# Agent attention with a maxout network: the first product over two PSUM tiles, w_out behind group 0's loads, and own orders for the last four groups

## The chip, the cores and the metric

The kernel runs on one core of a Trainium2 chip. The metric is device time in microseconds (us), the median of repeated executions. Engines are named as in the profile: PE is TensorE (PEld its weight loads), DVE is VectorE, ACT is ScalarE, POOL is GpSimd, SP is SyncE, which here only issues DMAs.

## The reference

Two stages. Attention goes through 49 agents for each of 4 batches of 12544 rows of 128 numbers; its result feeds a maxout network with 768 hidden units.

```python
def sm(a, b):
    s = scale * (a @ b.transpose(0, 2, 1))
    s = s - s.max(-1, keepdims=True)
    e = np.exp(s)
    return e / (e.sum(-1, keepdims=True) + 1e-09)
agent_v = sm(agents, k) @ v          # 49 x 128 for each batch
x = sm(q, agents) @ agent_v          # 50176 x 128 in all
h = np.maximum(np.maximum(x @ w1, x @ w2), x @ w3)
out = h @ w_out
```

## The kernel before

**What is multiplied.** The kernel never forms x. Because x is the agents' weights times agent_v, it multiplies agent_v (held turned, as avT) once for each batch with a wide matrix `wall`. That matrix has columns C21 to Dff for w2 - w1, C31 to C1O for w3 - w1 (but w3 - w2 for hidden block FI = 3), and from C1O for w1 times w_out, the linear part. The result of a batch is the tile G[b]. In `product` (lines 408 to 429) each product is a pair of matmuls, one for each half of the partitions, followed by a copy out of PSUM into G. A maximum of three is then rebuilt as a linear part plus sums of maxima: for each of the six hidden blocks f, `first(f)` (u) and `second(f)` (v) are matmuls of G with the exponentials of the scores (line 533). `relu_first` (a, line 548) runs on ACT and `max_second` (x, line 558) on DVE. For f = FI both steps are on ACT (lines 545 and 556), in the same PSUM tile. `out_linear` (line 563) and `out_hidden` (oc0f and oc1f for the two halves of a group, line 572) sum into an output tile, and `out_scale` (sc0, sc1, line 579) multiplies by the reciprocal row sums on its way to SBUF. `store` (line 586) writes a whole group once both scales are done.

**Stages.** The 392 row tiles are handled in 49 groups of eight. Batch 0's keys and values come first, alone, in twelve "early" groups (9 tiles each, the last two 4 each). Their last sums give avT for batch 0 (`normalise`, lines 402 and 403), and product 0 follows. Keys and values of batches 1 to 3 are worked on beside the query groups 0 to 35. Groups 36 to 48 have query work alone and use DMA transposes.

**Order.** Every step is put on one list with a key, by `at(key, fn, name, needs, ring, frees)`. `emit` sorts by key. A step whose needs are not yet done, or whose ring of PSUM buffers has none free, waits on a second list and is taken as soon as it can. What comes out is the program order of each engine's instructions, and each engine keeps to that order. The rings are "uv" (three tiles of two banks), "om" (two tiles of one bank) and "a" (three SBUF tiles). For a query group the keys are 6.0 times the group's number plus an entry of a table: KEY, BEGIN and BORDER for the groups with keys beside them, LATE for the rest (`table`).

**What the change touches.** `load_w_out` (line 193) is put at last_key - 29.85, right behind the load of query group 0 (last_key - 29.9) and ahead of the loads of key group 0 (at -24.6). w_out isn't in the ring of load tiles. `prep_w_out` (line 222) casts it on POOL at last_key - 3.24, behind the cast of query group 1 (last_key - 3.25). `linear_out` (line 240) and `linear_product_out` (line 249) copy the linear part out of PSUM on ACT. In `k_tail` batch 0's product has two pieces, (C31, C31 + 256, C1O) and (C21, C31). The first piece is one tile with two copies between its matmuls, and its key of last_key + 0.95 comes after the scores of group 0 at last_key + 0.94. The transposes of key group 0 (line 294) have last_key + 1.05, and the first u follows at last_key + 2.

Of the kernel before, what the change touches and what calls it, by code (L numbers as in the profile page):

```python
# [11 lines left out]
AF = mybir.ActivationFunctionType  # L12
# [4 lines left out]
def kernel(  # L17
# [18 lines left out]
    nc = tc.nc  # L36
    B, N, C = q.shape
    A = agents.shape[1]
    Dff = moe_w1.shape[1]
    scale = 1.0 / math.sqrt(C)  # L40
    P = 128
    NF = Dff // P
    H = 64
# [5 lines left out]
    NQ = B * NT // GT  # L49
# [46 lines left out]
        "oc11": 11.381, "oc13": 11.497,  # L96
    }
    PRODUCT_KEYS = (-8.717, -1.818)
    BEHIND = 2.6

    def table(s):
        if s + 1 in tails:
            return BORDER
        return BEGIN if s in tails and s < SB else KEY if s < SB else LATE
# [6 lines left out]
    def uv_tile(dtype=FP32):  # L111
        return psum.tile([P, 2, 512 if dtype == FP32 else 1024], dtype, tag="uv", bufs=3, name="uv_ps")
# [6 lines left out]
    def at(key, fn, name=None, needs=(), ring=None, frees=()):  # L119

        ops.append((key, len(ops), fn, name, needs, ring, frees))
# [46 lines left out]
    avT = const.tile([P, B, H], BF16, name="avT")  # L170
# [3 lines left out]
    r_ag = const.tile([P, B], FP32, name="r_ag")  # L174
# [25 lines left out]
    C21, C31, C1O = 0, Dff, 2 * Dff  # L200
    wall = const.tile([P, 2 * Dff + 3 * C], BF16, name="wall")
    nc.vector.memset(wall[:, C1O:], 0.0)
    WC = 2 * Dff + 2 * C
# [26 lines left out]
    linear = {}  # L230
# [4 lines left out]
    def prep_linear1(f):  # L235
        nc.tensor.matmul(linear["t"][:, :C], w1T[:, f, :], wo_bf[:, f, :], start=(f == 0),
                         stop=(f == NF - 1))

    def linear_out():
        nc.scalar.activation(wall[:, C1O + C:C1O + 2 * C], linear["t"][:, :C], AF.Copy)  # L240

    def linear_product():
        for h in range(2):
# [2 lines left out]
                             start=False, stop=True, skip_group_check=True)  # L246

    def linear_product_out():
        nc.scalar.activation(G[0][:, C1O:WC], linear["t"][:, C:3 * C], AF.Copy)

    def keep_busy(times):
        t = small_tile("m_ps")
# [4 lines left out]
    G = {}  # L257
# [6 lines left out]
    def k_group(b, t0, n, key, s):  # L264

        d = {}
        early = s is None
        K = None if early else table(s)
        if s == 0:
            key += BEHIND  # L270

# [110 lines left out]
    def k_tail(b, sum_key, keys, s):  # L382
        d = {}

        def reduce():
            w = KT // 2 * A
            t = Eacc[b]
            while w >= A:
                nc.gpsimd.tensor_tensor(out=t[:, :w], in0=t[:, :w], in1=t[:, w:2 * w], op=ALU.add)
                w = w // A // 2 * A  # L390
            nc.gpsimd.tensor_tensor(out=e_sum[:, :A], in0=t[:, :A], in1=t[:, KT * A - A:], op=ALU.add)

        def total():
            for h in range(2):
                nc.tensor.matmul(host[s][h * H:(h + 1) * H, :1], e_sum, ones[:, :1], start=True,
                                 stop=True, skip_group_check=True)

        def normalise():
            if s is None:

                r = last_tile["t"][:, :A]
                nc.vector.reciprocal(r, Vacc[b][:, A:])
                nc.vector.tensor_tensor(out=avT[:, b, :A], in0=Vacc[b][:, :A], in1=r, op=ALU.mult)
            else:
                nc.vector.reciprocal(r_ag[:, b:b + 1], host[s][:, :1])
            G[b] = work.tile([P, WC], BF16, tag="G", name="G")

        def product(c0, *ends):

            t = uv_tile().rearrange("p i c -> p (i c)")  # L410

            at0 = c0 if len(ends) == 1 else ends[0] - 512
            a = c0
            for z in ends:
                cuts = sorted({a, z} | {c for c in (at0 + 512, C1O) if a < c < z})
                for lo, hi in zip(cuts, cuts[1:]):
                    for h in range(2):


                        c = lo + (C if lo >= C1O and h == 0 else 0)  # L420
                        nc.tensor.matmul(t[h * H:(h + 1) * H, lo - at0:hi - at0], avT[:, b, :],
                                         wall[:, c:c + hi - lo], start=True, stop=True,
                                         skip_group_check=True)
                src = t[:, a - at0:z - at0]
                if s is None:
                    nc.vector.tensor_copy(out=G[b][:, a:z], in_=src)  # L426
                else:
                    nc.scalar.activation(G[b][:, a:z], src, AF.Copy, scale=r_ag[:, b:b + 1])
                a = z

        if s is not None:
            at(6.0 * (s - 1) + table(s - 1)["ke"] + 1.51, reduce, ("sum_e", b), [("kx", s - 1)])
            at(sum_key + 0.8, total, ("total", s), [("sum_e", b), ("ho", s)])
        at(sum_key + 0.81, normalise, ("normalise", b),
           [("ka", ("early", NT - last_size))] if s is None else [("total", s), ("ka", s - 1)])

        pieces = ((C31, C31 + 2 * P, C1O) if s is None else (C31, WC), (C21, C31))
        for i, piece in enumerate(pieces):
            at(keys[i], lambda piece=piece: product(*piece),
               ("product", b, i), [("normalise", b)], "uv", [("product", b, i)])  # L440


    def split(t0, t1, step):
# [10 lines left out]
    def q_group(s):  # L454
# [4 lines left out]
        d = {}  # L459
# [28 lines left out]
        def evacuate():  # L488
# [4 lines left out]
            else:  # L493
                nc.scalar.activation(qT, d["qT_ps"], AF.Copy)  # L494

        K = table(s)
        q_dma = s >= SB or s + 1 in tails

# [76 lines left out]
        def out_scale(o):  # L575
            if "out" not in d:
                d["out"] = work.tile([P, GT, C], FP32, tag="o_sb", bufs=3, name="o_sb")
            j, m = 2 * pairs[o][0], 2 * len(pairs[o])
            nc.vector.tensor_tensor(  # L579
                out=d["out"][:, j:j + m, :],  # L580
                in0=d["o", o].rearrange("p (j c) -> p j c", c=C),
                in1=d["r"][:, j:j + m].unsqueeze(2).to_broadcast([P, m, C]), op=ALU.mult)
# [8 lines left out]
        def put(name, fn, *needs, ring=None, frees=()):  # L591
            at(key + K[name] + (BEHIND if s == 0 and name in ("sum", "rec") else 0), fn, (name, s), needs,
               ring, frees)
# [30 lines left out]
        for f in range(NF):  # L624
            def each(fn, f=f):
                return lambda: fn(f)
            u, a, v, x = (n + str(f) for n in "uavx")
# [8 lines left out]
        for o in range(2):  # L636
            put(f"lin{o}", lambda o=o: out_linear(o), ("ex", s), *new_linear, ring="om",
                frees=[(f"sc{o}", s)])
            for f in range(NF):
                put(f"oc{o}{f}", lambda o=o, f=f: out_hidden(o, f), (f"lin{o}", s), (f"x{f}", s))  # L640
            put(f"sc{o}", lambda o=o: out_scale(o), ("rec", s),
                *[(f"oc{o}{f}", s) for f in range(NF)], *([("store", s - 3)] if s >= 3 else []))
        at(key + 12.2, store, ("store", s), [("sc0", s), ("sc1", s)])

    def ramp():

        at(KEY["lin1"] - 6, linear_tile, "linear", ["lin_a"], "om", ["lin_c"])
        keys = sorted(KEY[f"oc1{f}"] for f in range(NF))
        for f, key in enumerate(keys):
            at(key - 6, lambda f=f: prep_linear1(f), ("linear", f), ["linear"])  # L650
        key = 6 + KEY["a0"] + 0.01
        at(key, linear_out, "linear_out", [("linear", f) for f in range(NF)])
        at(key + 0.4, linear_product, "lin_b", ["linear_out"])
        at(6 + KEY["a1"] + 0.01, linear_product_out, "lin_c", ["lin_b", ("normalise", 0)])

# [1 line left out]
    last_key = KEY["u0"] - 2  # L659
# [3 lines left out]
    at(first_key - 6.5, load_weights)  # L663
    at(first_key + 30.2, prep_weights)
    at(first_key + 37.1, prep_linear0, "lin_a", (), "om", ["lin_a"])
    at(last_key - 29.85, load_w_out)
    at(last_key - 3.24, prep_w_out)
    fillers = []
    for g, n in enumerate(first_sizes):
        k_group(0, sum(first_sizes[:g]), n, first_key + 6.0 * g, None)  # L670

        if 4 <= g < len(first_sizes) - 3:
            fillers += [(first_key + 6.0 * g + 0.55, 3), (first_key + 6.0 * g + 1.3, 3)]
    k_tail(0, last_key, (last_key + 0.95, last_key + 1.02), None)
    for key, n in fillers + [(last_key + 0.9, 2), (KEY["u1"] + 0.01, 2),
                             (KEY["u3"] + 0.05, 2)]:
        at(key, lambda n=n: keep_busy(n), ("busy", key), (), "om", [("busy", key)])
    hosting = set()
    for b in range(1, B):
        for g in range(NK):  # L680
            s = (b - 1) * NT // GT + g
            hosting.add(s)
            k_group(b, g * KT, min(KT, NT - g * KT), 6.0 * s, s)
    for s, b in tails.items():
        assert s - 1 not in hosting
        k_tail(b, 6.0 * (s - 1) + table(s - 1)["ho"] + 0.001, [6.0 * s + PRODUCT_KEYS[i] for i in range(2)], s - 1)
    for s in range(NQ):
        q_group(s)
    ramp()

    with tc.manual_schedule():
# [31 lines left out]
```

## Time and profile before

| | |
|---|---|
| median of 8 executions | 463.36 us (463.18 to 463.49) |
| the profiled execution | 463.31 us |
| its span, first to last instruction | 461.5 us |
| granted TensorE clock | 0.999 of full |
| one group with keys beside it (68.72 to 77.08) | 8.36 us |
| one group without (424.88 to 432.74) | 7.86 us |
| last scale ends, end of the span | 457.92, 461.5 us |

The profile gives busy time for each engine. A busy PE is not a PE at its peak, since matmuls overlap and their ends are modelled. So the table gives starts: a step's cost in the stream is the distance from its start to that of the next one. Three stretches matter: up to about 41 us the loads of batch 0's keys and values set the pace; from 41 to about 62 us the query groups start up; then comes a regular run of groups to about 440 us, and the last groups drain.

### The profile page before, as it was taken

What the parts mean: (1) busy time and instruction counts of PE and PEld (TensorE: products, weight loads), DVE (VectorE), ACT (ScalarE), POOL (GpSimd) and SP (SyncE); (2) the same over time, 40 slices, a digit from 0 to 9 for tenths busy, and PEclk for the clock granted to TensorE, in tenths of its full rate; (3) what the DMA queues carried; (4) which work ended last, traced back from release to release, by engine and by line L of the source; (5) the groups of instructions that cost most, each with busy time, mean ns of one, the idle gap of its engine ahead of it and who ended that gap; (6) DMA issues with size and microseconds to landing.
All of it is one profiled execution on the core that took longest, in us unless ns stands there. A gap on an engine that the chain in (4) does not pass through costs nothing.

```text
span 461.5 us, 13320 instructions
## 1 busy us (share of the span) xinstructions
PE 437.4 (95%) x5457; PEld 274.4 (59%) x5462; DVE 402.2 (87%) x510; ACT 396.6 (86%) x460; POOL 171.8 (37%) x179
## 2 busy tenths in 40 slices
PE   2598899999999999999999999999999999999996
PEld 2476466666656666666656666666656555555554
DVE  3255899999989999999989999999988999999995
ACT  3365989999899899898998998999999999999982
POOL 2244964644462535445273355363240101100000
PEclk9999999999999999999999999999999999999999
DMA  8999999999999999998987999996776485644122
GB/s 314 408 410 391 349 343 355 334 343 253 311 318 289 289 291 311 293 260 254 319 304 265 274 302 323 300 249 191 159 148 184 126 196 150 182 116 125 60 94 91
DMA packets 82632, 118.53 MB, mean 257 GB/s; under 512 B 56391, under 2 KB 57867, under 8 KB 82571
## 3 DMA queue, kind: packets, MB, share of 16 engines
q1 hardware_dynamic: 82368, 117.59, 83.8%
q8 instruction: 42, 0.69, 0.6%
q14 instruction: 19, 0.16, 0.1%
q10 hardware_dynamic: 203, 0.10, 0.1%
HBM read 78.74 MB, written 25.69 MB: 226 GB/s over the span
## 4 chain that ended last, share of the span: by engine, by line
PE 80%; DMA 8%; DVE 5%; ACT 4%; issue 1%; SPq 0%; POOL 0%; DVEq 0%; ACTq 0%
PE uv_ps L533 34%; PE o_ps L572 29%; PE o_ps L563 6%; DMA st<-in_k_dram 5%; PE m_ps L486 4%; DVE r L558 4%; PE m_ps L507 3%; ACT a_sb L548 2%; DMA st<-in_q_dram 2%; DMA st<-in_v_dram 2%; PE m_ps L323 2%; PE m_ps L312 1%; PE m_ps L521 1%; DVE o_sb L579 0%; DVE G L426 0%
## 5 line engine op out<-in xcount | busy, mean ns | idle before, releaser
L558 DVE TENSOR_TENSOR r<-uv_ps,a_sb 128x1024 bf16<-128x1024 f32 x245 | 297.6, 1221 | 16.3 <-PE uv_ps L533 7.6
L548 ACT ACTIVATE a_sb<-uv_ps 128x1024 bf16<-128x1024 f32 x245 | 241.0, 1028 | 15.4 <-PE uv_ps L533 13.9
L533 PE MATMUL uv_ps<-e_q,G 49*128 49x512 bf16 (+3 forms) x1248 | 186.8, 368 | 2.5 <-ACT a_sb L548 0.3
L572 PE MATMUL o_ps<-wo_bf,r 128*128 128x128 bf16 x2352 | 175.2, 220 | 0.2 <-DVE r L558 0.2
L572 PEld LDWEIGHTS <-r 128*128 128x128 bf16 x2352 | 137.7, 98 | 40.1 <-issue 38.1
L533 PEld LDWEIGHTS <-G 49*128 49x128 bf16 x1248 | 57.7, 93 | 64.7 <-issue 32.7
L342 POOL TENSOR_TENSOR Eacc<-Eacc,e_k 128x441 f32<-128x441 f32 (+1 forms) x30 | 30.5, 1017 | 124.8 <-ACT e_k L317 124.8
L579 DVE TENSOR_TENSOR o_sb<-o_ps,recips 128x512 f32<-128x512 f32 x98 | 67.5, 689 | 9.1 <-PE o_ps L572 6.3
L481 POOL CAST q_bf<-st 128x1024 bf16<-128x1024 f32 x49 | 50.9, 1042 | 61.7 <-DMA qT<-q_bf 59.1
L556 ACT ACTIVATE r<-uv_ps 128x1024 bf16<-128x1024 f32 x49 | 50.2, 1025 | 17.9 <-PE uv_ps L533 17.7
L280 POOL CAST k_bf<-st 128x1152 bf16<-128x1152 f32 (+2 forms) x45 | 50.4, 1121 | 29.3 <-DMA st<-in_k_dram 23.2
L545 ACT ACTIVATE uv_ps<-uv_ps 128x1024 f32<-128x1024 f32 x49 | 49.6, 1013 | 0.2
L563 PE MATMUL o_ps<-G,e_q 128*128 128x256 bf16 x196 | 38.0, 276 | 0.0
L287 POOL CAST v_bf<-st 128x1152 bf16<-128x1152 f32 (+1 forms) x33 | 37.5, 1136 | 0.6 <-DMA st<-in_v_dram 0.6
L513 ACT ACTIVATE e_q<-m_ps 128x512 bf16<-128x512 f32 x49 | 29.9, 610 | 0.5 <-PE m_ps L507 0.5
L285 ACT ACTIVATE v_bf<-st 128x1152 bf16<-128x1152 f32 (+1 forms) x12 | 12.9, 1073 | 13.2 <-DMA st<-in_v_dram 13.1
L563 PEld LDWEIGHTS <-e_q 128*128 128x128 bf16 x196 | 12.5, 97 | 18.7 <-issue 18.0
L300 DVE COPY kT<-uv_ps 128x1152 bf16<-128x1152 bf16 (+1 forms) x14 | 9.9, 709 | 14.6 <-PE uv_ps L294 14.6
L486 PEld LDWEIGHTS <-q_bf 128*128 128x128 bf16 x264 | 14.9, 98 | 13.0 <-issue 11.1
L492 DVE COPY qT<-m_ps 128x1024 bf16<-128x1024 bf16 x32 | 21.8, 682 | 0.0
L486 PE MATMUL m_ps<-ident,q_bf 128*128 128x128 bf16 x264 | 20.4, 220 | 0.3 <-POOL q_bf L481 0.3
L507 PE MATMUL m_ps<-qT,agT 128*64 128x512 bf16 (+3 forms) x104 | 19.9, 388 | 0.7 <-ACT qT L494 0.7
(71 smaller groups left out, 227.4 us busy)
## 6 DMA issues: line engine op xcount, KB each, us to landing
st<-in_q_dram SPq DMA_DIRECT2D x46, 512.0 KB, 4.7
out_dram<-o_sb SPq DMA_DIRECT2D x46, 512.0 KB, 3.7
st<-in_k_dram SPq DMA_DIRECT2D x40, 576.0 KB, 6.7
st<-in_v_dram SPq DMA_DIRECT2D x40, 576.0 KB, 7.4
st<-in_k_dram SPq DMA_DIRECT2D x3, 512.0 KB, 6.2
st<-in_v_dram SPq DMA_DIRECT2D x3, 512.0 KB, 7.2
wst<-in_moe_w_dram SPq DMA_DIRECT2D x3, 384.0 KB, 10.5
st<-in_q_dram SPq DMA_DIRECT2D x2, 384.0 KB, 4.6
```

The lines of the kernel that those rows point to most:

```text
L280: nc.gpsimd.tensor_copy(out=d["kb"][:, :n, :], in_=d["k"][:, :n, :])
L287: nc.gpsimd.tensor_copy(out=d["vb"][:, :n, :], in_=d["v"][:, :n, :])
L481: nc.gpsimd.tensor_copy(out=d["qb"], in_=d["q"])
L486: nc.tensor.transpose(t[:, j * P:(j + 1) * P], d["qb"][:, j, :], ident)
L533: nc.tensor.matmul(t[:, h, j0 * P:j1 * P], G[b][h * H:h * H + A, col + f * P:col + (f + 1) * P], d["e"][h * H:h * H + A, j0 * P:j1 * P], s ...
L545: nc.scalar.activation(u, u, AF.Relu)
L548: nc.scalar.activation(a_sb[f], u, AF.Relu)
L556: nc.scalar.activation(r, v_ps[f], AF.Relu)
L558: nc.vector.tensor_tensor(out=r, in0=v_ps[f], in1=a_sb[f], op=ALU.max)
L563: nc.tensor.matmul(t[:, i * 2 * C:(i + 1) * 2 * C], d["e"][:, jj * P:(jj + 1) * P], G[batch[jj]][:, C1O:C1O + 2 * C], start=(i == 0), stop ...
L572: nc.tensor.matmul(t[:, c:c + C], r_sb[f][:, h, jj * P:(jj + 1) * P], wo_bf[:, f, :], start=False, stop=True, skip_group_check=True)
L579: nc.vector.tensor_tensor(out=d["out"][:, j:j + m, :], in0=d["o", o].rearrange("p (j c) -> p j c", c=C), in1=d["r"][:, j:j + m].unsqueeze( ...
```

## The change

Six things change.

1. Batch 0's product is three steps. `product_first` writes columns C31 to C31 + 256 into one tile and copies them; `product_second` writes 512 columns from there and 512 from C21 into a second tile and copies each; `product_third` writes the remaining 256 columns into the free half of the first tile and copies them. The first two have keys ahead of the first scores, the third behind them.
2. The load of w_out goes from ahead of key group 0's loads to behind its keys and values.
3. The cast of w_out on POOL goes ahead of the cast of query group 1.
4. The two copies of the linear part go from ACT to DVE, the second one with an earlier key.
5. The last four groups (45 to 48) each have a table of their own instead of LATE.
6. In the last group the scale of the second half of the output (o = 1) is four ACT instructions instead of one of DVE.

The products of batches 1 to 3 stay as they were, in a shorter function.

```diff
+    LAST = [
...
+    ]
     def table(s):
+        if s >= NQ - len(LAST):
+            return LAST[s - NQ]
...
     def linear_out():
-        nc.scalar.activation(wall[:, C1O + C:C1O + 2 * C], linear["t"][:, :C], AF.Copy)
+        nc.vector.tensor_copy(out=wall[:, C1O + C:C1O + 2 * C], in_=linear["t"][:, :C])
...
     def linear_product_out():
-        nc.scalar.activation(G[0][:, C1O:WC], linear["t"][:, C:3 * C], AF.Copy)
+        nc.vector.tensor_copy(out=G[0][:, C1O:WC], in_=linear["t"][:, C:3 * C])
...
+        def multiply(t, at0, a, z):
+
+            cuts = sorted({a, z} | {c for c in (a - at0 + 512, C1O) if a < c < z})
+            for lo, hi in zip(cuts, cuts[1:]):
+                for h in range(2):
+                    c = lo + (C if lo >= C1O and h == 0 else 0)
+                    nc.tensor.matmul(t[h * H:(h + 1) * H, at0 + lo - a:at0 + hi - a], avT[:, b, :],
+                                     wall[:, c:c + hi - lo], start=True, stop=True,
+                                     skip_group_check=True)
...
+        cut = C31 + 2 * P
+
+        def product_first():
+            t = d["p"] = uv_tile().rearrange("p i c -> p (i c)")
+            multiply(t, 0, C31, cut)
+            nc.vector.tensor_copy(out=G[b][:, C31:cut], in_=t[:, :cut - C31])
+
+        def product_second():
+            t = uv_tile().rearrange("p i c -> p (i c)")
+            multiply(t, 0, cut, C1O)
+            multiply(t, 512, C21, C21 + 512)
+            nc.vector.tensor_copy(out=G[b][:, cut:C1O], in_=t[:, :C1O - cut])
+            nc.vector.tensor_copy(out=G[b][:, C21:C21 + 512], in_=t[:, 512:])
+
+        def product_third():
+            multiply(d["p"], 512, C21 + 512, C31)
+            nc.vector.tensor_copy(out=G[b][:, C21 + 512:C31], in_=d["p"][:, 512:512 + C31 - C21 - 512])
...
-        pieces = ((C31, C31 + 2 * P, C1O) if s is None else (C31, WC), (C21, C31))
...
+        if s is None:
+            at(keys[0], product_first, ("product", 0, 0), [("normalise", 0)], "uv", [("product", 0, 2)])
+            at(keys[0] + 0.001, product_second, ("product", 0, 1), [("product", 0, 0)], "uv",
+               [("product", 0, 1)])
+            at(keys[1], product_third, ("product", 0, 2), [("product", 0, 0)])
...
             j, m = 2 * pairs[o][0], 2 * len(pairs[o])
+            if s == NQ - 1 and o == 1:
+
+                for i in range(m):
+                    nc.scalar.activation(d["out"][:, j + i, :], d["o", o][:, i * C:(i + 1) * C], AF.Copy,
+                                         scale=d["r"][:, j + i:j + i + 1])
+                return
...
-        at(6 + KEY["a1"] + 0.01, linear_product_out, "lin_c", ["lin_b", ("normalise", 0)])
+        at(6 + KEY["ka"] + 0.01, linear_product_out, "lin_c", ["lin_b", ("normalise", 0)])
...
-    at(last_key - 29.85, load_w_out)
-    at(last_key - 3.24, prep_w_out)
+    at(-24.55, load_w_out)
+    at(last_key - 3.28, prep_w_out)
...
-    k_tail(0, last_key, (last_key + 0.95, last_key + 1.02), None)
+    k_tail(0, last_key, (last_key + 0.93, last_key + 1.02), None)
```

LAST holds one table for each of groups 45, 46, 47 and 48, with the same names as LATE. A few of their keys, those of the last group among them:

```diff
+        {"v3": -164.4181, "x5": -156.2085, "oc14": -101.5261, "sc0": -56.4089, "a4": -33.1221,
...
+        {"a4": -135.5952, "s": -3.6850, "ex": -2.2030, "ho": -1.9346, "u0": -1.3390,
+         "sum": -0.9715, "a0": 0.1977, "rec": 0.3166, "u1": 1.4697, "u2": 3.5883, "v1": 3.7970,
+         "a1": 3.8096, "u3": 3.9647, "a2": 5.0765, "a3": 5.2628, "x1": 6.1940, "v0": 6.2913,
+         "v2": 6.3762, "v3": 6.7820, "x0": 10.4629, "sc1": 11.0558, "x3": 12.8641, "u4": 13.1350,
+         "v4": 13.7666, "x2": 16.1146, "u5": 19.9425, "v5": 20.9765, "sc0": 27.0577,
+         "x4": 27.8299, "oc04": 43.1860, "a5": 44.1320, "oc15": 44.9180, "lin1": 46.2961,
+         "oc13": 49.5958, "oc11": 49.9320, "oc12": 50.9170, "oc10": 55.9318, "oc14": 57.5404,
+         "oc05": 60.1508, "lin0": 70.3912, "oc03": 74.0752, "oc00": 92.6315, "oc01": 97.6449,
+         "x5": 102.3830, "oc02": 107.1067},
```

## The prediction

> **What bounds the kernel now.** I read the page first, then busy time by stretch, then the chain of waits and the timeline of the two ends.
>
> ```profile
> span 461.5 us, 13320 instructions
> PE 437.4 (95%) x5457; PEld 274.4 (59%) x5462; DVE 402.2 (87%) x510; ACT 396.6 (86%) x460; POOL 171.8 (37%) x179
> ...
> PE 80%; DMA 8%; DVE 5%; ACT 4%; issue 1%; SPq 0%; POOL 0%; DVEq 0%; ACTq 0%
> ```
>
> The reader is to see that the chain that ends last lies on TensorE for 80%. The profiled run took 463.31 us, 1.8 outside its span; the median is 463.36, so sums made on the span carry over. By stretch (us, then busy time of PE, PEld, DVE, ACT, POOL):
>
> ```profile
> 424.90:432.80 7.90, 7.87 (x86) 4.44 (x85) 7.33 (x9) 7.37 (x9) 0.00 (x0) 1.00 0.37 103
> 440.70:448.50 7.80, 7.66 (x82) 4.39 (x81) 7.21 (x9) 6.98 (x9) 0.00 (x0) 1.00 0.18 68
> 448.50:452.00 3.50, 3.17 (x35) 1.68 (x33) 3.20 (x4) 2.50 (x4) 0.00 (x0) 1.00 0.35 143
> 452.00:455.00 3.00, 2.79 (x42) 2.27 (x41) 2.85 (x3) 0.94 (x2) 0.00 (x0) 1.00 0.00 0
> 455.00:461.50 6.50, 2.19 (x38) 1.99 (x35) 1.49 (x3) 0.00 (x0) 0.00 (x0) 0.94 0.40 161
> ```
>
> One late group (7.9 us) leaves PE no idle time, DVE 0.57 and ACT 0.53: three engines nearly full, PE first. Only the last 20 us have gaps. The chain at the front:
>
> ```profile
> 43.48 0.41 PE m_ps L507 x2
> 43.89 0.12 PE uv_ps L421 x2
> ...
> 44.04 0.44 DVE G L426
> ...
> 44.52 0.42 PE uv_ps L421 x2
> ...
> 44.96 1.57 DVE G L426 x2
> ...
> 46.57 0.39 PE uv_ps L533 x2
> ```
>
> The first product of batch 0 (L421) goes behind the first scores (L507); its second part then waits for the first copy (L426), and the second hidden block (L533) for the last copy. What stands beside it, in the timeline:
>
> ```profile
> 44.03 1.15 POOL L280 CAST k_bf<-st 128x1152 bf16<-128x1152 f32 x1 [2.33 <-PE uv_ps L421]
> ...
> 45.23 0.68 PE L294 MATMUL uv_ps<-ident,k_bf 128*128 128x128 bf16 x9
> ...
> 45.84 0.39 PE L533 MATMUL uv_ps<-e_q,G 49*128 49x512 bf16 x2
> ...
> 46.70 1.04 POOL L481 CAST q_bf<-st 128x1024 bf16<-128x1024 f32 x1
> ```
>
> Group 0's key cast starts at 44.03. Its named releaser is accidental: the program gives it no wait on L421, and its load, issued at 35.13 behind w_out, lands about then. So PE's transposes of it come at 45.23 and the first hidden block at 45.84. The tail:
>
> ```profile
> 452.15 2.36 DVE L558 TENSOR_TENSOR r<-uv_ps,a_sb 128x1024 bf16<-128x1024 f32 x2 [0.39 <-PE uv_ps L533]
> ...
> 454.57 1.07 PE L572 MATMUL o_ps<-wo_bf,r 128*128 128x128 bf16 x16 [0.21 <-DVE r L558]
> ...
> 455.69 1.50 PE L572 MATMUL o_ps<-wo_bf,r 128*128 128x128 bf16 x24
> 457.23 0.69 DVE L579 TENSOR_TENSOR o_sb<-o_ps,recips 128x512 f32<-128x512 f32 x1 [0.87 <-PE o_ps L572]
> ```
>
> After the last maximum (ends 454.51) PE still has 40 output matmuls and two linear ones; the last scale follows, and the store takes 3.6 us to the end.
>
> **What the Trainium skill says.** "TensorEngine Tiling (Array Packing)", Key Properties: changing the tiling mode drains TensorE. The trace agrees: hidden matmuls (49*128) and output ones (128*128) alternate; a block of six hidden ones takes 0.76 us (440.60 to 441.36), a block of two 0.32 (446.17 to 446.49), so 0.11 for each matmul and 0.1 for the change of kind. "ScalarE: Activation LUTs", What ACT_TABLE_LOAD costs: a pointer operand adds about 93 ns to an ACTIVATE, and back-to-back ones overlap by about as much. Here 128x1024 takes 1028 ns without the pointer (L548) and 1115 with it (L428), and two of L548 take 1.94. "DMA: Bandwidth & Descriptors", HWDGE ordering: on each DMA engine descriptors are consumed in ring order, though completion is not strictly first-in first-out. Loads between 30 and 50 us landed in 8.3 to 11.6 us, at a steady 400 GB/s.
>
> **Product, scores, keys of group 0.** avT is ready at 42.73 (L403 ends), qT at 43.43. The new first product waits for avT with the scores queued behind it; it needs 0.11 us of streaming, the second product 0.43, so both are issued by 43.4 and the scores still start at 43.48: cost nothing, and at most 0.1 if the drain shows. Copies on DVE: 256 columns 0.43 from 43.13, two of 512 at 0.69 each, then the third product's 256, 0.43: end about 45.35, against 46.53. Four copies cost 2.24 against 2.07 before, hidden because they begin 0.9 earlier and the 0.5 wait between them goes (the second product has its own tile).
>
> w_out moves behind k0 and v0. It never held a load buffer, so k0 lands by w_out's share earlier: 384 KB at 400 GB/s is 1.0 us; I take 42 to 43. The cast (1.15) ends by 44.1, and PE turns the keys right behind the third product, near 44.1. The first hidden block then waits only for the first tile, which the third product holds to the fourth copy: 45.37 instead of 45.84. The second follows at 45.6 instead of 46.57. ACT's first relu moves from 46.27 to 45.77.
>
> **What is late next.** PE's in-order queue comes to the transposes of q group 1, whose cast began at 46.70. Its load stands behind the same bytes as before, so it doesn't come earlier; with the w_out cast (0.83) now ahead of it on POOL it starts at 46.7 if w_out lands by 45.8. I put w_out's landing at 45.4 (v0's of before: the same bytes). The transposes go from 48.41 to about 47.9. From there ACT is full to 58 us (3.63 of 4.00 busy from 48 to 52, 3.96 of 4.00 after), so the 0.5 stays.
>
> **Linear copies to DVE.** ACT loses L240 (0.27) and L249 (0.40). DVE gains a 128-column copy, estimated at 0.29 from the 256 (0.43) and 512 (0.69) copies, and a 256 copy, 0.43. DVE has one gap here of 0.67 (56.05 + 0.16 to 56.88); behind the copies stand a reciprocal, an add and the next maximum. The sum of 0.72 fills the gap, so DVE moves by 0.45 where ACT could move by 1.1. From both sides: a loss of 0.3 to a gain of 0.5; I take zero. The front as a whole: 0.5 gained (0 to 1.0). From 62 us the chain is PE without a break, so the shift reaches the end. The key of the w_out cast alone costs nothing: its first reader is at 53.39.
>
> **The last four groups.** I sorted the keys into the order that emit() gives. From group 44's last hidden tiles to the end PE has 27 hidden blocks before and 26 after: group 45 gets one more (v4 and u0 split by an output piece), groups 46 and 47 keep theirs, the last group has two fewer. A hidden block less is two changes less: +0.2 in group 45, then -0.4. PE's waits before are 0.17 (446.8), 0.39 (448.6), 0.4 (454.1) and some smaller: about 1.0.
>
> New last group, PE: u2 v1 u3, outputs, v0 v2 v3, outputs, u4 v4, outputs, u5 v5, then one output of group 47, lin1, five oc1, lin0, four oc0, and only then the three that need maximum 5. By the durations above: scores of group 48 at 440.5; maximum 5 of group 47 ends 447.2, so v1 waits 0.4; u3 done 447.7; maximum 1 ends 449.0, v0 v2 v3 done 449.5; u4 v4 at 450.8; u5 v5 at 452.1, done 452.5; ACT's relu 5 ends 453.5. DVE before the last maximum: maximum 4 to 453.5, the moved sc0 of group 47 (0.69) to 454.2, maximum 5 to 455.4. That is 0.9 later than 454.51, but PE has 12 matmuls left instead of 42: 0.64 and 0.15 drain, 456.2; sc0 ends 456.95. The other scale is four ACTIVATEs of 128x128: 0.273 (L240) plus 0.09, overlapped, 1.17 in all from 455.85: 457.0. So the store is issued at 457.0 instead of 457.9: 0.9 gained (a loss of 0.5 to a gain of 1.5, since nothing of before shows this order). Were the four on DVE, they would add 0.5.
>
> Sum: 463.31 - 0.5 - 0.9 = 461.9.
>
> **Rivals.**
> (a) The front gives nothing. k0 may land no earlier, or the PE order may still wait for q group 1's cast; the 512-byte rows of w_out speak for it (lands late, holds POOL), the steady 400 GB/s against. Then 463.31 - 0.9 = 462.4.
> (b) Both ends give all: ACT's relief carries through (1.0) and the tail comes to PE's waits and switches, 1.2: 461.1. For it, ACT's load at 48 to 58; against, DVE's gap is exactly filled.
> (c) Slower: the last group starves on the three uv buffers. u2 v1 u3 and v0 v2 v3 wait for maxima on DVE in series (5 of 47, 1, 0, 2). I cover each wait to within 0.2 to 0.4; if each of three costs a whole maximum less its cover (1.22 - 0.3), the last maximum ends near 458.2 and not 455.4. It costs 2.8 against 1.4 gained: 464.7. It decides from a last maximum later than 456.8 on the old clock. Against it: DVE work from 444.0 to that maximum sums to 10.7, which allows 454.7.
>
> **How the numbers follow.** Forecast 0.48, (a) 0.21, (b) 0.18, (c) 0.13. The measurement can tell about 0.2% (0.9 us) from no change: below 462.4 is faster. The forecast's own range, 461.2 to 462.6, puts 0.42 of its 0.48 there; (a) sits on the bound, 0.08 of it faster, 0.12 same and 0.01 slower; (b) all faster. With (c) slower: faster 0.68, same 0.18, slower 0.14. The range reaches from under (b), 460.6, to 463.3, where (a) ends; (c) is left out.
>
> **What would show it.** Right: L421 ahead of L507 and starting at 42.8; key cast of group 0 before 43; first L533 near 45.4; first reading of q group 1 on PE before 48.1; the piece at 70 us earlier by 0.5; 12 output matmuls after the last maximum; ACT scales beside DVE's. Wrong: w_out's cast after 47, DVE idle over 1 us in the last 15, or the steady period of groups 3 to 44 changed, for nothing of the change touches it.

## The result and the profile after

The changed kernel took 460.99 us (median of 10, 460.79 to 461.26) against 463.42 for the kernel before on the same chip: a ratio of 0.9948 with a 95% interval of 0.9940 to 0.9956. It is faster by 2.4 us, inside the predicted range and 0.9 below the predicted 461.9. The profiled execution took 460.79.

The page of the changed kernel, with the same lines as were shown of before:

```profile
span 459.0 us, 13326 instructions
PE 436.2 (95%) x5457; PEld 273.9 (60%) x5462; DVE 402.1 (88%) x512; ACT 397.5 (87%) x462; POOL 171.9 (37%) x179
...
PE 81%; DMA 10%; DVE 4%; ACT 3%; issue 1%; POOL 0%; ACTq 0%; SPq 0%; DVEq 0%
```

The span is 2.5 us shorter and no engine has less work to speak of: DVE has two instructions more (three copies more, one scale less), ACT two (four scales, less two copies). The time comes from when things happen, and only the traces' clocks show where. I call shift the start of an instruction less the start of the same one in the kernel before. At the output scales of groups 1, 13, 37 and 46 it is -1.22 us each time, and at the end of the span -2.5. So the front gave 1.22, the 40-odd groups between nothing, and the tail the other 1.3.

The front in the timeline of the changed kernel (start, duration, engine, line, operation, idle time before it and its releaser). The product is L456 now, its copies L471 to L482, the hidden blocks L590, the transposes of keys L334, of queries L543:

```profile
42.21 1.15 POOL L320 CAST k_bf<-st 128x1152 bf16<-128x1152 f32 x1 [0.49 <-DMA st<-in_k_dram]
...
42.85 0.73 PE L456 MATMUL uv_ps<-wall,avT 128*64 128x256 bf16 x6
...
43.51 0.41 PE L564 MATMUL m_ps<-qT,agT 128*64 128x512 bf16 x2
...
43.95 0.68 PE L334 MATMUL uv_ps<-ident,k_bf 128*128 128x128 bf16 x9
...
44.97 0.72 PE L590 MATMUL uv_ps<-e_q,G 49*128 49x512 bf16 x4 [0.34 <-DVE G L478]
...
45.16 0.83 POOL L262 CAST wo_bf<-wo_st 128x768 bf16<-128x768 f32 x1
...
45.40 1.94 ACT L605 ACTIVATE a_sb<-uv_ps 128x1024 bf16<-128x1024 f32 x2 [0.85 <-PE uv_ps L590]
...
46.48 1.04 POOL L538 CAST q_bf<-st 128x1024 bf16<-128x1024 f32 x1 [0.49 <-DMA st<-in_q_dram]
...
47.58 0.62 PE L543 MATMUL m_ps<-ident,q_bf 128*128 128x128 bf16 x8 [0.17 <-POOL q_bf L538]
```

The product now runs ahead of the scores (43.51; 43.48 before), group 0's keys are cast 1.8 us earlier, and the first two hidden blocks come in one run from 44.97. Then two releasers name what is late next: query group 1's cast waits for its DMA, and PE's transposes for that cast. The chain of waits of the changed kernel starts there too:

```profile
37.40 9.02 DMA st<-in_q_dram
...
46.48 1.05 POOL q_bf L538
...
47.58 0.64 PE m_ps L543 x8
...
48.23 0.58 DVE qT L549
...
48.85 1.24 DVE r L615
```

In the kernel before, the copies of the product (DVE G L426) stood on this chain. Now a load does. The tail, in the timeline of the changed kernel:

```profile
452.51 1.22 DVE L615 TENSOR_TENSOR r<-uv_ps,a_sb 128x1024 bf16<-128x1024 f32 x1
452.70 0.38 PE L620 MATMUL o_ps<-G,e_q 128*128 128x256 bf16 x2
452.92 1.73 PE L629 MATMUL o_ps<-wo_bf,r 128*128 128x128 bf16 x28
...
454.24 1.14 ACT L639 ACTIVATE o_sb<-o_ps,recips 128x128 f32<-128x128 f32 x4 [2.19 <-PE o_ps L629]
...
454.69 0.69 DVE L642 TENSOR_TENSOR o_sb<-o_ps,recips 128x512 f32<-128x512 f32 x1 [0.96 <-PE o_ps L629]
```

PE goes through its last matmuls beside the last maximum (452.51 to 453.73) with no wait of its own, and the two scales run beside each other and end at 455.38. In the kernel before the last scale ended at 457.92.

### The profile page after: what moved, and what is told of

Its sections match the earlier page's. It is cut to its first block, busy times and chain, and to the rows that moved or that the text cites. A ratio compares the mean times of both kernels' runs of the same rounds, so it can differ in the third digit from the quotient of the medians.

```text
span 459.0 us, 13326 instructions
## 1 busy us (share of the span) xinstructions
PE 436.2 (95%) x5457; PEld 273.9 (60%) x5462; DVE 402.1 (88%) x512; ACT 397.5 (87%) x462; POOL 171.9 (37%) x179
## 4 chain that ended last, share of the span: by engine, by line
PE 81%; DMA 10%; DVE 4%; ACT 3%; issue 1%; POOL 0%; ACTq 0%; SPq 0%; DVEq 0%
PE uv_ps L590 34%; PE o_ps L629 30%; PE o_ps L620 6%; DMA st<-in_k_dram 5%; PE m_ps L543 4%; DVE r L615 4%; PE m_ps L564 3%; DMA st<-in_v_dram 2%; DMA st<-in_q_dram 2%; ACT a_sb L605 2%; PE m_ps L363 2%; PE m_ps L352 1%; DMA ag_st<-in_agents_dram 1%; PE m_ps L578 1%; ACT G L463 0%
## 5 line engine op out<-in xcount | busy, mean ns | idle before, releaser
L590 PE MATMUL uv_ps<-e_q,G 49*128 49x512 bf16 (+3 forms) x1248 | 186.4, 368 | 1.8 <-DVE G L478 0.3
L590 PEld LDWEIGHTS <-G 49*128 49x128 bf16 x1248 | 57.9, 93 | 64.1 <-issue 31.5
L613 ACT ACTIVATE r<-uv_ps 128x1024 bf16<-128x1024 f32 x49 | 50.2, 1025 | 19.3 <-PE uv_ps L590 19.0
L543 PEld LDWEIGHTS <-q_bf 128*128 128x128 bf16 x264 | 14.8, 98 | 13.3 <-issue 11.1
L543 PE MATMUL m_ps<-ident,q_bf 128*128 128x128 bf16 x264 | 20.4, 220 | 0.4 <-POOL q_bf L538 0.4
```

Of the source, the lines that this page charges most:

```text
L543: nc.tensor.transpose(t[:, j * P:(j + 1) * P], d["qb"][:, j, :], ident)
L590: nc.tensor.matmul(t[:, h, j0 * P:j1 * P], G[b][h * H:h * H + A, col + f * P:col + (f + 1) * P], d["e"][h * H:h * H + A, j0 * P:j1 * P], s ...
L613: nc.scalar.activation(r, v_ps[f], AF.Relu)
```

## The experiments

All medians are in us; "before" is the kernel before on the same chip.

```
run                     time     before   ratio  95% interval      span
tail_only               461.84   463.29   0.9969 0.9957 to 0.9980  460.1
head_only               461.97   463.29   0.9972 0.9961 to 0.9984  460.2
linear_on_act           461.27   463.29   0.9957 0.9943 to 0.9970  459.3
scale_on_dve            460.76   463.29   0.9945 0.9932 to 0.9957  458.9
product_old             462.45   463.25   0.9983 0.9976 to 0.9989  460.6
w_out_early             460.99   463.25   0.9955 0.9941 to 0.9968  459.2
w_out_alone             463.19   463.25   1.0000 0.9991 to 1.0008  461.4
w_out_later             460.41   463.25   0.9938 0.9926 to 0.9951  458.5
changed_again           460.58   463.34   0.9941 0.9929 to 0.9954  458.9
product_alone           462.74   463.34   0.9987 0.9980 to 0.9993  460.7
w_out_later_scale_dve   460.50   463.34   0.9939 0.9925 to 0.9953  458.8
own_order_last_only     468.18   463.34   1.0106 1.0091 to 1.0122  466.4
```

And the start of the work in each trace. The second column is query group 1's cast on POOL, the third PE's transposes of it, the fourth the first ACT pass that is late after them (group 1's hidden block FI, second pass; L613, L556 in the kernel before), the fifth the fourth less the third:

```
run                     q1 cast  q1 transposes  FI pass  FI less transposes
kernel before           46.70    48.41          59.04    10.63  linear copies on ACT
w_out_alone             46.89    48.43          59.08    10.65  on ACT
tail_only               46.27    48.43          59.08    10.65  on ACT
product_alone           46.35    47.77          58.40    10.63  on ACT
linear_on_act           46.37    47.47          58.10    10.63  on ACT
product_old             46.56    48.40          58.64    10.24  on DVE
w_out_early             46.40    47.87          58.12    10.25  on DVE
changed kernel          46.48    47.58          57.82    10.24  on DVE
own_order_last_only     46.77    47.87          58.12    10.25  on DVE
w_out_later             45.28    47.15          57.40    10.25  on DVE
```

The last column takes two values only, and it goes by the engine of the linear copies: their move is worth 0.39 us, whatever else is changed. The rest of the front is the third column.

**Do the two ends add?** tail_only is the kernel before with the four tables and the last group's ACT scale; head_only is the changed kernel without these:

```diff
-        if s >= NQ - len(LAST):
-            return LAST[s - NQ]
...
-            if s == NQ - 1 and o == 1:
```

> The kernel before with only the own tables of the last four groups and the last scale on ACT. The traces put the two kernels 1.21 us apart when the last scores are issued and 2.5 apart at the end, so if front and tail simply add, this one gains 1.3 us on the kernel before (ratio 0.9972). If the tail's gain comes only because the front ran ahead (loads or stores further away), it gains clearly less, below 0.7.

> The changed kernel with LATE for the last four groups and both last scales on DVE: the front's parts alone. If they add: 1.2 us faster than before (ratio 0.9974). If the new tables also shorten groups 45 to 47, less than 1.0 is left for the front.

Measured: 1.45 less than before for the tail and 1.32 for the head, together 2.77, where the changed kernel has 2.43 on its chip and 2.76 in changed_again. The two ends are separate and add, within what two chips differ. Both are worth more than the forecast's 0.9 and 0.5, but some 0.35 of the tail's gain may come from a hold in the kernel before, an idle time that nothing in the profile explains, and not from the order (see the end).

**The linear copies.** linear_on_act puts both copies back on ACT, with the old key of the second:

```diff
-        nc.vector.tensor_copy(out=wall[:, C1O + C:C1O + 2 * C], in_=linear["t"][:, :C])
+        nc.scalar.activation(wall[:, C1O + C:C1O + 2 * C], linear["t"][:, :C], AF.Copy)
...
-        nc.vector.tensor_copy(out=G[0][:, C1O:WC], in_=linear["t"][:, C:3 * C])
+        nc.scalar.activation(G[0][:, C1O:WC], linear["t"][:, C:3 * C], AF.Copy)
...
-        at(6 + KEY["ka"] + 0.01, linear_product_out, "lin_c", ["lin_b", ("normalise", 0)])
+        at(6 + KEY["a1"] + 0.01, linear_product_out, "lin_c", ["lin_b", ("normalise", 0)])
```

> The changed kernel with the two linear copies back on ACT at the old key. Theory: ACT is what limits from 48 to 58 us, its relief of 0.67 carries through by 0.3 to 0.5, so this one ends 0.4 us later than the changed kernel (about 461.4). Rival, as the prediction took it: DVE loses as much as ACT gains, no difference (within 0.1). In the trace the second pass on ACT over block FI of group 1 should then come at 58.2 or later instead of 57.82.

Measured: 461.27, 0.5 above scale_on_dve on the same chip, which has the copies on DVE. Of this, 0.37 stands at the FI pass (58.10 against 57.73 in scale_on_dve). The rest is not the copies': linear_on_act loses 0.12 each at two places further on (108 and 235 us, see the end), and its tail is the shorter one (by shift 1.4 us gained against 1.2). First the timeline of linear_on_act, then that of the changed kernel, whose clock is 0.11 behind here (47.58 against 47.47):

```profile
54.88 0.27 ACT L280 ACTIVATE wall<-o_ps 128x128 bf16<-128x128 f32 x1
...
55.93 1.23 DVE L615 TENSOR_TENSOR r<-uv_ps,a_sb 128x1024 bf16<-128x1024 f32 x1 [0.66 <-PE uv_ps L590]
...
58.10 1.02 ACT L613 ACTIVATE r<-uv_ps 128x1024 bf16<-128x1024 f32 x1 [0.84 <-PE uv_ps L590]
```

```profile
55.01 0.28 DVE L280 CAST wall<-o_ps 128x128 bf16<-128x128 f32 x1
55.21 0.20 DVE L584 RECIPROCAL recips<-m_ps 128x8 f32<-128x8 f32 x1
55.32 0.16 DVE L375 TENSOR_TENSOR Vacc<-m_ps,Vacc 128x49 f32<-128x49 f32 x1
55.69 0.42 DVE L289 CAST G<-o_ps 128x256 bf16<-128x256 f32 x1 [0.20 <-PE o_ps L285]
56.08 1.23 DVE L615 TENSOR_TENSOR r<-uv_ps,a_sb 128x1024 bf16<-128x1024 f32 x1
...
57.82 1.02 ACT L613 ACTIVATE r<-uv_ps 128x1024 bf16<-128x1024 f32 x1 [0.58 <-PE uv_ps L590]
```

The two copies fit into DVE's gap of 0.66: in the stream they take 0.20 (55.01 to 55.21) and 0.39 (55.69 to 56.08), and the next maximum comes 0.04 later (8.50 after the transposes against 8.46). ACT is free sooner and its FI pass, counted from the transposes, comes 0.39 earlier. The ACT side decides, as the forecast's upper bound had it.

**The last scale.** scale_on_dve leaves the block for o = 1 away, so that both scales of the last group are on DVE:

```diff
-            if s == NQ - 1 and o == 1:
-                for i in range(m):
-                    nc.scalar.activation(d["out"][:, j + i, :], d["o", o][:, i * C:(i + 1) * C], AF.Copy,
-                                         scale=d["r"][:, j + i:j + i + 1])
-                return
```

> The changed kernel with the last group's second half scaled on DVE. DVE's two scales of 0.69 would follow each other: the first can start when the last-but-eight output matmul is done, 454.2, the second at 454.9, so the store is issued at about 455.6 instead of 455.4: 0.2 us later (461.2). If PE's last matmuls were the only limit there is no difference; if four ACTIVATEs were the worse choice it is faster.

Measured: 460.76 at 463.29 before, a ratio no worse than that of the changed kernel. The timeline of scale_on_dve shows why so little is lost:

```profile
454.04 1.29 DVE L636 TENSOR_TENSOR o_sb<-o_ps,recips 128x512 f32<-128x512 f32 x2 [0.51 <-PE o_ps L629]
```

Two scales on DVE take 1.29 together, and the second can't start before PE's last matmul in either kernel. By shift (end of the span less group 46) the tail is worth 1.2 here and in w_out_later_scale_dve, and 1.3 in four kernels with the ACT scale (the changed kernel, changed_again, w_out_early and w_out_later; 1.4 in linear_on_act and tail_only). So it is worth about 0.1, less than the times can tell; the expectation of 0.2 was too high. The gain of the tail is not ACT's scale; it lies in the order of work, less the hold named above.

**The product alone, and all but the product.** product_old puts the old pieces and the old `product` back into the changed kernel; product_alone has only the new product:

```diff
-            at(keys[0], product_first, ("product", 0, 0), [("normalise", 0)], "uv", [("product", 0, 2)])
...
+        pieces = ((C31, C31 + 2 * P, C1O) if s is None else (C31, WC), (C21, C31))
...
-    k_tail(0, last_key, (last_key + 0.93, last_key + 1.02), None)
+    k_tail(0, last_key, (last_key + 0.95, last_key + 1.02), None)
```

> The changed kernel with batch 0's product in two pieces again, behind the first scores. The keys of group 0 are then on time (cast at 42.2), but the last copy into G ends at 46.5 as before, and the second hidden block waits for it. Theory: both the product and the keys were late before, either alone holds the first hidden blocks, so undoing this one gives back 0.5 us or more (461.5 to 461.9). Rival: only the keys mattered, nothing is given back (within 0.15).

> The kernel before with only batch 0's product in three steps. Taking single parts away left the front 0.28 (linear copies), 0.28 (w_out) and 0.8 us (product) later at 69 us. If the parts add, the product alone brings 0.65 us (462.7); if w_out's move is needed for it, because the keys' transposes stay at 45.0 ahead of the hidden blocks, 0.3 or less.

Measured: product_alone gains 0.60, near the 0.65 expected, and its transposes of query group 1 come 0.64 earlier. product_old stands only 0.8 below the kernel before, where the changed kernel stands 2.4 below. Half of these 1.6 us is the front (shift -0.41 at group 1 against -1.22), which fits the theory; the other half comes further on and isn't shown to have to do with the product. Its keys are cast as early as in the changed kernel (42.17), and still PE comes to the transposes of query group 1 at 48.40, as in the kernel before. Its timeline:

```profile
46.56 0.39 PE L572 MATMUL uv_ps<-e_q,G 49*128 49x512 bf16 x2 [0.39 <-DVE G L466]
...
373.30 1.23 DVE L597 TENSOR_TENSOR r<-uv_ps,a_sb 128x1024 bf16<-128x1024 f32 x1 [0.30 <-PE uv_ps L572]
```

The second hidden block stays behind the copies of the one tile, and everything behind it in PE's queue stays too. What is left of its front is the 0.4 of the linear copies. The second line is one of the three places further on (175, 373 and 446 us) where this kernel loses another 0.2, 0.35 and 0.35; the cause was not found (see the end).

**w_out's load.** Three places for it: the old one with the new product (w_out_early), the new one with the old product (w_out_alone), and one place further back, behind the load of query group 1 (w_out_later):

```diff
-    at(-24.55, load_w_out)
-    at(last_key - 3.28, prep_w_out)
+    at(-19.9, load_w_out)
+    at(last_key - 3.24, prep_w_out)
```

The other two have last_key - 29.85 and last_key - 3.24 put for the first two lines in the changed kernel, and the reverse in the kernel before.

> The changed kernel with the load and cast of w_out where they were. Theory: group 0's key cast is back at 44.0, PE's transposes of it at 45.2, first hidden block at 45.8 behind them though G is ready at 43.6: 0.6 to 0.8 us given back (461.6 to 461.8). Rival: the product alone made the gain, and then nothing is given back.

> The kernel before with only the load and cast of w_out moved. If either lateness alone holds the start, this gains little: the last copy of G still ends at about 46.5, so the second hidden block stays at 46.57, below 0.4 us gained. If the keys of group 0 were the one late thing, it gains 0.8 or more.

> The changed kernel with w_out loaded behind query group 1 too and cast behind it. In the changed kernel the chain now runs through that load (lands 46.42), its cast and PE's transposes at 47.58. Theory: it lands 1.0 us earlier, the transposes come at about 47.1 behind the filler matmuls, and ACT, idle for 0.2 at 48.4, closes that gap: 0.2 to 0.4 us faster than the changed kernel (460.6 to 460.8). Rival: ACT's and DVE's own work is the limit there, no difference. Its first reader is at 52.6, so lateness of w_out itself costs nothing in either.

The move alone gives nothing. The timeline of w_out_alone:

```profile
42.20 1.15 POOL L280 CAST k_bf<-st 128x1152 bf16<-128x1152 f32 x1 [0.49 <-DMA st<-in_k_dram]
...
45.20 0.68 PE L294 MATMUL uv_ps<-ident,k_bf 128*128 128x128 bf16 x9
...
46.59 0.39 PE L533 MATMUL uv_ps<-e_q,G 49*128 49x512 bf16 x2 [0.39 <-DVE G L426]
```

The keys are ready at 43.35 and PE takes them at 45.20, for they stand behind the old product in its queue. With the new product the order turns, in the timeline of w_out_early:

```profile
44.99 0.68 PE L334 MATMUL uv_ps<-ident,k_bf 128*128 128x128 bf16 x9 [0.95 <-POOL k_bf L320]
```

Now PE waits 0.95 for the cast. But the transposes of query group 1 come only 0.29 later (47.87 against 47.58), not the 0.6 to 0.8 that I expected, and the time can't tell it from the changed kernel. Nor can the traces: own_order_last_only, with w_out in its new place, has 47.87 too. So the move of w_out is not shown to bring anything, alone or with the new product. A reason is in w_out_later, first on POOL and then on PE:

```profile
45.28 1.04 POOL L538 CAST q_bf<-st 128x1024 bf16<-128x1024 f32 x1
...
46.55 0.83 POOL L262 CAST wo_bf<-wo_st 128x768 bf16<-128x768 f32 x1 [0.23 <-DMA wo_st<-in_moe_w_out_dram]
```

```profile
47.15 0.61 PE L543 MATMUL m_ps<-ident,q_bf 128*128 128x128 bf16 x8
```

With w_out behind it, query group 1's load lands so that its cast starts at 45.28 instead of 46.48, and PE gets to the transposes at 47.15 with no wait. In the kernel before, w_out's load stood ahead of both key group 0's and query group 1's. The change takes it out of the way of the first and leaves it in the way of the second, which is cast at 46.48 instead of 46.70; so what the early keys win ends at the next load. By shift w_out_later has 1.64 to 1.76 from group 1 to group 46, where the two traces of the changed kernel have 1.19 to 1.28.

**Does the later w_out beat the changed kernel?** changed_again is the changed kernel as it is, w_out_later_scale_dve has both edits, and they share a chip.

> The changed kernel unaltered, so that the three beside it are compared on one chip: 461.0, ratio 0.9948.

> The two edits that were not slower than the changed kernel, together: w_out behind query group 1, last scale on DVE. w_out_later was 0.5 us under the changed kernel; the DVE scale 0.1 to 0.2. If they add, 460.3; if the scale's 0.1 was the difference between chips, 460.45, same as w_out_later.

Measured: 460.58 (460.53 to 460.73) and 460.50 (460.49 to 460.59), and w_out_later had 460.41 elsewhere. The traces say that the front is 0.3 to 0.5 better with the later w_out; the intervals of the ratios overlap. No version was shown to beat the changed kernel.

**The last table without its neighbours.** own_order_last_only gives group 48 its own table and leaves LATE to groups 45 to 47:

```diff
-        if s >= NQ - len(LAST):
+        if s >= NQ - 1:
```

> The changed kernel with LATE for groups 45 to 47 and the own table for group 48 alone. The traces show the same shift of 1.21 at groups 44, 45, 46 and 47, so the three tables bring nothing by themselves: 461.0, no difference (within 0.15). If they prepare the last group (the output pieces of 47 that are deferred past its last hidden blocks, the table's own ring order), this one loses 0.3 or more.

Measured: 468.18 (466.96 to 469.17), 7.2 over the 460.99 of the changed kernel and 7.6 over changed_again on the same chip. The first theory fell. The second, that the three tables prepare the last group, had the right direction, but its "0.3 or more" gave no idea of the size. Stretches of its last 20 us (us, then busy time of PE, PEld, DVE, ACT, POOL with instructions, PE clock, DMA share, GB/s), then two lines of its timeline:

```profile
432.80:440.70 7.90, 7.71 (x85) 4.32 (x83) 7.55 (x9) 6.83 (x8) 0.00 (x0) 1.00 0.18 71
440.70:448.50 7.80, 5.54 (x66) 3.65 (x63) 5.25 (x7) 4.12 (x5) 0.00 (x0) 1.00 0.04 14
```

```profile
447.75 0.38 PE L620 MATMUL o_ps<-G,e_q 128*128 128x256 bf16 x2 [1.21 <-DVE o_sb L642]
...
454.44 0.61 PE L590 MATMUL uv_ps<-e_q,G 49*128 49x512 bf16 x4 [1.59 <-DVE r L615]
```

In the second stretch no engine is busy for more than 71% of it. The scores of the last group come at 441.39 (439.05 in the changed kernel), behind 16 output matmuls of group 46. Hidden blocks of group 48 then stand behind outputs of group 47, and PE waits for a scale to free its output tile (1.21) and for a maximum to free a uv tile (1.59), while DVE and ACT wait for PE. A key means a place among its neighbours' keys. In the changed kernel groups 45 to 47 keep the period of 7.86 between their scores (shift -1.22, -1.22 and -1.21 at groups 46, 47 and 48), so their three tables bring no time of their own: they make the fourth one work.

## Why the prediction was right, and where its sums were off

Right in direction and in the kind of both gains, by its own signs: product ahead of the scores at 42.85 (42.8 foretold), keys cast at 42.21 (42 to 43), w_out's cast at 45.16 (before 47), query group 1 on PE at 47.58 (before 48.1), an unchanged period in the groups between, 12 output matmuls after the last maximum, and ACT's scales beside DVE's. One sign of being wrong is met by the letter: in the last 15 us DVE is idle for 1.64 up to the last scale. But 0.96 of it is that scale's wait for PE's last matmuls, and only 0.68 lies between 444.00 and the end of the last maximum. The shift at 70 us was to be 0.5 and is 1.22; the end was to give 0.9 and gave 1.3. Both terms were too small, and the sum stayed inside the range because the range reached to rival (b): the number that came out, 460.99, is that of (b), 461.1, and so is part of its reason.

- **Product, scores, keys.** The first hidden block was set at 45.37, behind the fourth copy; it came at 44.97, behind the third (L478 ends at 44.91). Its columns are in the first copy, so what it waited for is a tile: by these times it took that of the second product, which the third copy frees, and the second hidden block (45.29) that of the first, which the fourth copy frees (L482 ends at 45.24). None of this 0.4 arrives: the next wait covers it. Group 0's keys were to come 1.0 earlier, the time of w_out's bytes "at a steady 400 GB/s"; they were cast 1.8 earlier (42.21 for 44.03). The rate isn't steady in the kernel before, either: it dips while w_out loads (see the end). This cost the forecast nothing, since PE takes the keys at 43.95, where it said 44.1.
- **What is late next.** Rightly named: query group 1's transposes, behind its load. The term was 0.5 (48.41 to 47.9) and measured 0.83 (to 47.58), for the cast was set at 46.7 and came at 46.48. Runs with the same loads had 46.37 to 46.77, so 0.2 of this is how the load happens to land.
- **Linear copies: the main error.** Their bounds were a loss of 0.3 and a gain of 0.5, and zero was taken. DVE's loss was sized well: 0.72 in a gap of 0.67 was to cost it 0.05, and it lost 0.04. What failed is the step after that, which let DVE's stream decide what goes on: ACT's gain of 0.39 went through. With 0.83 this makes the 1.22 of the front. Rival (b) had the right reason here, for a front of 1.0.
- **The last groups.** Scales were foretold to end at 457.0; on the old clock (1.22 added) they ended at 456.60. The last maximum was set at 455.4 and ended at 454.95. Two steps ahead of it cost less: the wait of 0.4 for v1 wasn't there, as maximum 5 of group 47 ended at 446.6 instead of 447.2, and the change of kind added to group 45 (+0.2) didn't lengthen it. Of this lead of 0.6 (maximum 1 of the last group ended at 448.38, set at 449.0) 0.2 was left when v3 was done; the rest of the 0.45 came in steps of about 0.1 behind it. That the gain was 1.3 and not 0.9 may have another part: the last groups of the kernel before lose some 0.35 that isn't their order's (see the end). Of the "three that need maximum 5" only two need it (oc15 and oc05); oc02 has the latest key. The Trainium skill ("TensorEngine Tiling (Array Packing)", Key Properties) says that changing the tiling mode drains TensorE; the blocks' durations gave 0.1 for each change, but group 45 kept its 7.86 us with one change of kind more each way, so that price can't be added block by block.
- **ACT's scales.** 1.14 measured for 1.17. "ScalarE: Activation LUTs", What ACT_TABLE_LOAD costs, gives about 93 ns for a pointer operand; here a 128x128 ACTIVATE takes 361 to 375 ns with it and 273 without, 88 to 102 more, which agrees. But the gain of 0.5 over DVE was wrong: two DVE scales at once took 1.29.
- **Rivals.** (a) fell: both parts of the front give, but it was right that PE would still wait for query group 1's cast (0.17) and that w_out's load comes late. (c), starving uv buffers, fell for the change as it is (last maximum 454.95, its point 456.8), but such starving exists: own_order_last_only shows it, on output tiles too, in a kernel that takes 7 longer.

## What to carry to other kernels

When a copy moves from a full engine to one with a gap, cost both: here it fitted into the gap, and the engine that lost it set the gain. When a load is moved out of the way of one tile, look which load it still stands in front of. A hand-made order for one group is worth testing only together with the orders of the groups that interleave with it.

## What was not expected of the hardware

- **w_out costs more than its bytes.** It is 384 KB, 1.0 us at 400 GB/s, in rows of 512 bytes. Group 0's keys were cast at 43.59 to 44.03 in the four traces with it ahead and at 42.09 to 42.91 in the ten without; query group 1 at 46.37 to 46.89 with it ahead in its new place and at 45.28 and 45.40 without. Between the medians that is 1.55 for the keys and 1.17 for the queries. The DMA view from 30 to 50 us, in slices of 0.5 us, of the kernel before, the changed kernel and w_out_later:

```profile
GB/s 406 415 415 424 396 406 448 391 380 372 403 382 377 397 393 394 384 362 331 356 371 352 431 396 397 375 408 432 434 407 396 400 411 396 427 407 396 430 412 401
```

```profile
GB/s 406 424 406 424 406 406 415 419 375 374 381 404 377 397 401 417 388 430 409 417 415 402 359 336 347 353 378 399 390 397 415 438 379 403 418 418 410 401 421 392
```

```profile
GB/s 396 406 415 415 433 387 429 381 381 381 385 395 389 389 410 416 415 415 418 390 396 433 397 402 354 368 340 362 357 400 387 387 409 405 401 406 407 428 422 444
```

  A dip of some 12% stands at 38.5 to 41.0 in the first, at 41.0 to 43.5 in the second and at 42.0 to 44.5 in the third, so it goes along with w_out. "DMA: Bandwidth & Descriptors", Specifications, in the Trainium skill, puts the line rate at 512 bytes and more; here the core's rate fell to 331 to 378 GB/s while a load with rows of just that size ran, and the measurement decides. Other row sizes were not tried.
- **Small holds at single places.** product_old loses 0.2 at group 14 and 0.35 at group 38, linear_on_act and product_alone 0.12 to 0.14 each at 108 and 235 us, where neighbouring groups with the same instructions lose nothing. In product_old they seem to repeat: its 20 executions lie within 462.34 to 462.66. The first of them in the timeline of product_old, and the same maximum in the changed kernel:

```profile
175.26 1.22 DVE L597 TENSOR_TENSOR r<-uv_ps,a_sb 128x1024 bf16<-128x1024 f32 x1 [0.19 <-ACT a_sb L587]
```

```profile
174.29 1.23 DVE L615 TENSOR_TENSOR r<-uv_ps,a_sb 128x1024 bf16<-128x1024 f32 x1
```

  The releaser named is the ACT pass that ends at 175.13. In the changed kernel the same pass ends at 174.35, after its maximum has started, so the maximum doesn't need it: it waited for nothing that the profile shows. One such hold lies in the last groups of the kernel before. Its line, and that of the same maximum in product_alone, which runs these groups in the same order:

```profile
445.72 1.23 DVE L558 TENSOR_TENSOR r<-uv_ps,a_sb 128x1024 bf16<-128x1024 f32 x1 [0.37 <-PE uv_ps L533]
```

```profile
444.92 1.23 DVE L613 TENSOR_TENSOR r<-uv_ps,a_sb 128x1024 bf16<-128x1024 f32 x1
```

  product_alone has no gap there, and its shift grows from -0.45 at group 46 to -0.81 at the end. So the old order without the hold ends some 0.35 sooner, and the new order by itself may be worth nearer 0.95 than 1.3. This rests on one execution, the fastest of 21 (462.50 to 463.01); head_only, with the old order again, has its hold a step later, on ACT (0.29), and ends like the kernel before. What the holds depend on stays open, and with it some 0.9 us of what product_old lost.
